# Last product of an attention-and-MLP kernel by halves of each row's tokens, one 7.5 KB place and one transfer for a step's results, and a new table of priorities

## The chip, the cores and the metric

The kernel runs on one core of a Trainium2 chip. The metric is the device time of one execution in microseconds (us). An execution's profile gives a span, from the first to the last instruction of the program; the time of the same execution lies a little above its span.

## The reference, cut to what matters

```python
# attention: x is [4, 12480, 128], inducing is [32, 128]
def mab(q, kv):
    s = scale * (q @ kv.transpose(0, 2, 1))
    a = softmax(s)                      # over the last axis, 1e-9 in the denominator
    return a @ kv
h = mab(I, x)                           # [4, 32, 128]: 32 rows look at all 12480 tokens of a batch
y = mab(x, h)                           # [4, 12480, 128]: every token looks at the 32 rows of h
# MLP on all 49920 tokens
u = y @ w_in                            # 128 -> 2048
out = (u - tanh(u)) @ w_out             # 2048 -> 128
```

The kernel uses that a token's `y` is a mixture of the 32 rows of `h`: it runs the MLP to first order around a mean on the 32 rows and then mixes 32 results per token. A check of the error's bound at the end (`limit`) would send the program to an exact general version; with these inputs that branch is not taken.

## The kernel before, in words

Data lies transposed, 128 channels on the partitions. A batch `b` (0 to 3) has six steps `s` of 1920 tokens (`SG`, four rows of 480, `NQ` = 4, `SEG` = 480) and a seventh of 1024 (four rows of 256; 64 tokens are done twice and cut off at the store by `dup`).

`first(b)`, with `attend`: for each step the tokens `xT` (7.5 KB of each partition, a buffer of the tag `xT`) are loaded and the scores against `inducing` are formed (L339, PE) and moved to SBUF (L365, DVE). After the batch's maximum is known come the exponentials (L418, ACT), their transposition to `et` (L421, DVE) and the sum over tokens (L428, PE) against the same tokens in the other layout, `xn`. Those are loaded too (`in_xn`, and `in_xl` for the seventh step), or for the steps in `TURNED` made from `xT` by PE (L401, evicted at L407).

`linear(b)`: the MLP on the 32 rows of `h` (`hT_all`): L510 up, L522, `tanh` and a series, L564 down, L568; its result is a 128x128 matrix `P4` (copied at L570), two places in turn.

`second(b, s)`, with `b_chain`: for each step again, from the same `xT` in SBUF: scores against `h` (L339, PE), transposition (L613, DVE), maximum (L615, DVE), subtraction (L620, POOL), exponential (L623, ACT), sum in two stages (L628 POOL, L631 DVE), reciprocal (L634), scaling (L635, POOL), transposition to `bt` (L639, DVE). In batch 3 every second step takes an `xn` buffer for this instead of `be` and `bt`. Then the last product (L667, PE): four matmuls with `P4`, one for each 480-token row, into two PSUM tiles `o` of two banks each. Two evictions (L673) copy the tiles to SBUF, into `ot` (batches 0 to 2) or into a spare `xT` (batch 3). There a planner may give an eviction to DVE where ACT is busy; elsewhere it is ACT's. Each half is stored by a transfer of its own (480 KB, L678; for the seventh step one transfer for both, L682).

All DMAs are issued by SP, in one order. The order of every engine's instructions comes from `Plan.order`: each operation is added with an engine, a cost, what it reads and writes, and a priority; the planner goes through time with those costs, and on each free engine starts the ready operation with the lowest priority whose buffers (`PLACES`, counted by tag) are free. Where PE would stand idle by the plan it puts matmuls of `ident` by `ident` (L763) whose result nobody reads. The priorities come from `ORD`. What an engine really waits for is a semaphore that the recording layer attaches when it sees two instructions on one tile; the planner's own picture of buffers has no part in that.

Of the kernel before, what the change touches and what calls it, by code (L numbers as in the profile page):

```python
# [10 lines left out]
F32 = mybir.dt.float32  # L11
# [8 lines left out]
NQ = 4  # L20
# [11 lines left out]
PLACES = dict(xT=11, xn=5, s1=1, be=5, bt=2, et=4, ot=5, ps=3, o=2, bs=1, D=1, M4=1, P1=2, P4=2)  # L32

ORD = dict(first=(-205, 200, 455, 875), second=(435, 945, 825, 1020), fs=(16, 32, 18, 9), ss=(21, 111, 96, 66),
           lx=(-172, -293, -302, -223), ln=(-59, -169, -75, -65), lns=(9, 15, 74, 54), turn=(60, 5, 83, 66),
           keep=(-51, -123, -93, -38), q=(-585, -579, -656, -488), half=(-201, -211, -200, -148),
           late=(230, 429, 304, 278), guard=1422, win=-364, wout=-187, lwin=-64.5, lwout=431.5,
           store=(-298, -304, -262, -383), base=(38, 76, -6, 45))
# [150 lines left out]
def fused_kernel(ctx, tc, xT, xn, xl, indT, w_in, w_out, outT):  # L189
# [17 lines left out]
    ps_o = ctx.enter_context(tc.tile_pool(name="ps_o", bufs=2, space=PSUM))  # L207
# [15 lines left out]
    plan = Plan(PLACES)  # L223
# [26 lines left out]
    add("SP", 0.3, lambda: nc.sync.dma_start(out=indT_sb, in_=indT), writes=[ind_b], pri=-500, lag=2)  # L250
# [392 lines left out]
    def second(b, s, pri):  # L643
# [3 lines left out]
        full = not dup  # L647

        def out(bt, held):

            if b == B - 1:

                whole = io_buf("xT", [C, SG])
                ots = [Buf(lambda h=h: whole.get()[:, 2 * h * seg:2 * (h + 1) * seg]) for h in range(2)]
                keep = [whole]
            elif full:
                ots, keep = [io_buf("ot", [128, NQ * HEG]) for _ in range(2)], []
            else:
                whole = io_buf("ot", [128, NQ * HEG])
                ots = [Buf(lambda h=h: whole.get()[:, 2 * h * seg:2 * (h + 1) * seg]) for h in range(2)]  # L660
                keep = [whole]
# [9 lines left out]
            for h, (o, ot) in enumerate(zip(tiles, ots)):  # L671
                def ev(copy, o=o, ot=ot):
                    copy(out=ot.get()[:, :2 * seg].rearrange("p (q n) -> p q n", q=2), in_=o.get()[:, :, :seg])  # L673
# [202 lines left out]
```

## Time and profile before

| | |
|---|---|
| time, median of 3 runs (lowest to highest) | 205.13 us (202.23 to 206.51) |
| time of the profiled execution | 204.65 us |
| its span | 202.9 us |
| busy, share of the span | PE 85%, DVE 74%, ACT 58%, POOL 45% |
| DMA | 72.3 MB in the SP queue's transfers, 91% of the 16 engines' time |
| mean granted TensorE clock | 0.957 |

A line of the views names source line, engine, operation, and output<-inputs. "x8" behind L667 are the records of four matmuls: each of these 32-bit matmuls leaves two. "landing" is the time at which a transfer's data is there, counted from its issue. Busy times are sums over the named stretch; the clock is the share of full speed that TensorE was granted in it.

### The profile page before, as it was taken

How to read it: one execution, taken by the hardware profiler on the slowest of the kernel's cores; microseconds unless marked ns; L12 is line 12 of the kernel's file. 1: busy time of each engine (PE TensorE's matmuls, PEld its weight loads, DVE VectorE, ACT ScalarE, POOL GpSimd, SP SyncE). 2: the span in 40 equal slices, each digit the busy share in tenths (PEclk: the TensorE clock that was granted, in tenths of full speed). 3: DMA queues.
4: the chain of work that ended last, by engine and by line, in shares of the span. 5: the costliest groups of instructions: out<-in, count | busy, mean ns of one | idle time of the engine just before them, and what ended most of it. 6: DMA issues, size and time to landing. Idle time of an engine off the chain costs nothing.

```text
span 202.9 us, 5388 instructions
## 1 busy us (share of the span) xinstructions
PE 172.1 (85%) x2088; PEld 98.8 (49%) x2088; DVE 149.3 (74%) x398; ACT 117.3 (58%) x236; POOL 91.1 (45%) x138
## 2 busy tenths in 40 slices
PE   7769999898689897699869889999975999899950
PEld 7634478544455543234346644344545634476530
DVE  5799499889879975286569884895772149999950
ACT  2536599534463778248765824667982297585330
POOL 1052202223659366137228532898541017899400
PEclk9969999999999999699999999999997599999996
DMA  5999999999999999979999999999999776447993
GB/s 180 400 427 421 405 423 382 411 407 417 423 368 337 363 422 403 399 282 400 351 392 424 420 414 364 371 357 414 401 286 401 316 296 246 182 181 318 404 402 121
DMA packets 15581, 72.69 MB, mean 358 GB/s; under 512 B 1856, under 2 KB 1856, under 8 KB 15552
## 3 DMA queue, kind: packets, MB, share of 16 engines
q1 hardware_dynamic: 15552, 72.31, 91.0%
q8 instruction: 17, 0.28, 0.5%
q14 instruction: 12, 0.10, 0.1%
HBM read 46.74 MB, written 25.56 MB: 356 GB/s over the span
## 4 chain that ended last, share of the span: by engine, by line
DMA 41%; PE 39%; DVE 8%; ACT 3%; SPq 2%; issue 2%; POOL 0%; DVEq 0%; ACTq 0%
DMA xT<-in_xT 29%; PE ps_m L339 12%; PE bank L428 8%; PE o L667 8%; DMA outT<-ot 5%; DMA xn<-in_xn 4%; DMA xn<-in_xl 4%; PE ps_m L401 3%; PE bank L763 3%; DVE xT L673 2%; PE ps_m L510 1%; DVE xn L302 1%; PE ps_m L522 1%; SPq L287 1%; ACT xn L407 1%
## 5 line engine op out<-in xcount | busy, mean ns | idle before, releaser
L673 ACT COPY ot<-o 128x960 f32<-128x960 f32 (+1 forms) x42 | 37.1, 910 | 19.9 <-PE o L667 10.2
L339 PE MATMUL ps_m<-xT,indT_sb 128*32 128x480 f32 (+1 forms) x224 | 28.8, 586 | 11.3 <-DMA xT<-in_xT 10.8
L428 PE MATMUL bank<-xn,et 128*32 128x128 f32 x784 | 29.8, 286 | 4.0 <-DMA xn<-in_xn 3.2
L620 POOL TENSOR_TENSOR be<-be,bmx 128x480 f32<-128x480 f32 (+1 forms) x25 | 23.8, 952 | 16.7 <-DVE bmx L615 15.4
L428 PEld LDWEIGHTS bank<-xn,et 128*32 128x32 f32 x784 | 24.0, 114 | 13.5 <-issue 4.1
L635 POOL TENSOR_TENSOR be<-be,brs 128x480 f32<-128x480 f32 (+1 forms) x25 | 23.2, 934 | 14.3 <-DVE brs L634 12.9
L667 PE MATMUL o<-bt,P 32*128 32x480 f32 (+1 forms) x200 | 28.5, 600 | 0.5 <-ACT ot L673 0.4
L763 PE MATMUL bank<-ident 128*128 128x128 f32 x176 | 26.8, 297 | 1.8 <-POOL ident masks.py:199 1.3
L365 DVE TENSOR_SCALAR_CACHE_REDUCE s<-ps_m 128x480 f32<-128x480 f32 (+1 forms) x28 | 17.3, 620 | 14.7 <-PE ps_m L339 14.7
L763 PEld LDWEIGHTS bank<-ident 128*128 128x128 f32 x176 | 23.0, 203 | 8.3 <-issue 5.7
L407 ACT COPY xn<-ps_m 128x512 f32<-128x512 f32 (+1 forms) x36 | 19.1, 565 | 13.3 <-PE ps_m L401 13.1
L339 PE MATMUL ps_m<-xT,hT_all 128*32 128x480 f32 (+1 forms) x224 | 25.1, 545 | 0.6 <-ACT D L526 0.4
L628 POOL TENSOR_TENSOR bs<-be 128x240 f32<-128x240 f32 (+1 forms) x25 | 16.9, 678 | 19.0 <-ACT be L623 13.6
L401 PE MATMUL ps_m<-ident,xT 128*128 128x128 f32 x135 | 20.6, 291 | 1.8 <-DMA xT<-in_xT 1.6
L401 PEld LDWEIGHTS ps_m<-ident,xT 128*128 128x128 f32 x135 | 15.4, 147 | 12.6 <-issue 4.1
L418 ACT ACTIVATE s<-s,nb 128x480 f32<-128x480 f32 (+1 forms) x28 | 18.9, 676 | 2.2 <-DVE nb L387 2.2
L623 ACT ACTIVATE be<-be 128x480 f32<-128x480 f32 (+1 forms) x25 | 14.5, 579 | 9.6 <-POOL be L620 9.2
L639 DVE STREAM_TRANSPOSE bt<-be 128x480 f32<-128x480 f32 (+1 forms) x25 | 15.7, 628 | 4.2 <-PE o L667 3.7
L421 DVE STREAM_TRANSPOSE et<-s 128x480 f32<-128x480 f32 (+1 forms) x28 | 17.2, 622 | 1.8 <-ACT s L418 1.5
L613 DVE STREAM_TRANSPOSE be<-ps_m 128x480 f32<-128x480 f32 (+1 forms) x25 | 15.5, 624 | 3.3 <-PE ps_m L339 3.3
L312 POOL TENSOR_TENSOR wout_sb<-wout_sb,xn 128x512 f32<-128x512 f32 x4 | 5.1, 1276 | 22.9 <-DVE xn L308 22.9
L615 DVE TENSOR_REDUCE bmx<-be 128x15 f32<-128x480 f32 (+1 forms) x25 | 14.9, 596 | 0.2
(127 smaller groups left out, 221.4 us busy)
## 6 DMA issues: line engine op xcount, KB each, us to landing
xT<-in_xT SPq DMA_DIRECT2D x24, 960.0 KB, 10.3
outT<-ot SPq DMA_DIRECT2D x39, 480.0 KB, 8.1
xn<-in_xn SPq DMA_DIRECT2D x15, 960.0 KB, 8.7
outT<-xT SPq DMA_DIRECT2D x13, 480.0 KB, 3.4
xn<-in_w_in SPq DMA_DIRECT2D x4, 512.0 KB, 5.3
xT<-in_xT SPq DMA_DIRECT2D x4, 512.0 KB, 10.5
xn<-in_w_out SPq DMA_DIRECT2D x4, 512.0 KB, 5.7
xn<-in_xl SPq DMA_DIRECT2D x4, 512.0 KB, 8.2
```

Of the source, the lines that this page charges most:

```text
L339: nc.tensor.matmul(ps[q * m:(q + 1) * m, :seg], lhsT=w, rhs=row, start=True, stop=True)
L365: nc.vector.tensor_scalar(out=s1.get()[:, s, :seg], in0=ps.get()[:, :seg], scalar1=1.0, scalar2=None, op0=ALU.mult, op1=ALU.max, accum_out ...
L401: nc.tensor.transpose(out=pt.get()[:, i * 128:(i + 1) * 128], in_=xT_b[b, s].get()[:, (k + i) * 128:(k + i + 1) * 128], identity=ident)
L407: nc.scalar.copy(out=x.get()[:, k:k + n, :].rearrange("p k c -> p (k c)"), in_=pt.get()[:, :n * 128])
L418: nc.scalar.activation(out=sl, in_=sl, func=AF.Exp, scale=SC, bias=nb.get(), accum_out=sums.get()[:, s:s + 1])
L421: add("DVE", share(0.66, seg), lambda et=et, s=s, seg=seg, kb=kb: nc.vector.transpose(out=et.get()[:, :kb].rearrange("p k i -> p (k i)"), ...
L428: nc.tensor.matmul(hacc.get()[q * m:(q + 1) * m, :], lhsT=et.get()[:, k, :], rhs=x.get()[:, k, :], start=(s == group[0] and k < NQ), stop= ...
L620: add("POOL", share(1.02, seg), lambda: nc.gpsimd.tensor_tensor(out=be.get()[:, :kb], in0=be.get()[:, :kb], in1=wide(bmx.get()[:, :kb]), o ...
L635: add("POOL", share(1.02, seg), lambda: nc.gpsimd.tensor_tensor(out=be.get()[:, :kb], in0=be.get()[:, :kb], in1=wide(brs.get()[:, :kb]), o ...
L667: nc.tensor.matmul(tiles[q // 2].get()[:, q % 2, :seg], lhsT=P4_b[b].get()[p, :], rhs=bt.get()[p, :seg], start=True, stop=True)
L673: copy(out=ot.get()[:, :2 * seg].rearrange("p (q n) -> p q n", q=2), in_=o.get()[:, :, :seg])
L763: nc.tensor.matmul(bank[:, 2 * C:2 * C + 128], lhsT=ident, rhs=ident, start=first_fill, stop=True, skip_group_check=not first_fill)
```

## The change

The last product goes by halves of each row's tokens. Half A is tokens 0 to 239 of each of the four rows, half B tokens 240 to 479. One PSUM tile `four` of four banks is made once and kept; row `q` has bank `q`, with A in columns 0 to 239 and B in columns 256 to 495. Each half has four matmuls of 240 columns and an eviction of 4x240 elements per partition. For the planner A and B are two tags, `oA` and `oB`, with one place each. Both halves of a step go into one buffer of 7.5 KB, which one transfer of 960 KB stores (480 KB for the seventh step): 28 stores in place of 52.

Places: `ot` 5 of 4 KB before, 2 of 7.5 KB now; `xT` 11 to 12, `et` 4 to 2, `bt` 2 to 3. Every entry of `ORD` but `late`, `wout` and `base` has new numbers, and the load of `inducing` (`indT_sb`) stands behind the first load of `w_in`. `PLACES`, `ORD`, this load and `second` are all that is touched; line numbers behind the first lines shift by one, and behind `second` by eleven.

```diff
-PLACES = dict(xT=11, xn=5, s1=1, be=5, bt=2, et=4, ot=5, ps=3, o=2, bs=1, D=1, M4=1, P1=2, P4=2)
+PLACES = dict(xT=12, xn=5, s1=1, be=5, bt=3, et=2, ot=2, ps=3, o=2, bs=1, D=1, M4=1, P1=2, P4=2)
-           late=(230, 429, 304, 278), guard=1422, win=-364, wout=-187, lwin=-64.5, lwout=431.5,
-           store=(-298, -304, -262, -383), base=(38, 76, -6, 45))
+           late=(230, 429, 304, 278), guard=1440, win=-361, wout=-187, lwin=-96.5, lwout=346.5,
+           store=(-298, -311, -264, -383), base=(38, 76, -6, 45))
...
-    plan = Plan(PLACES)
+    plan = Plan(dict(PLACES, oA=1, oB=1))
...
+    four = ps_o.tile([128, NQ, 512], F32, name="four")
...
         def out(bt, held):
-            if b == B - 1:
-                whole = io_buf("xT", [C, SG])
-                ots = [Buf(lambda h=h: whole.get()[:, 2 * h * seg:2 * (h + 1) * seg]) for h in range(2)]
-                keep = [whole]
-            elif full:
-                ots, keep = [io_buf("ot", [128, NQ * HEG]) for _ in range(2)], []
...
-            tiles = [Buf(lambda: ps_o.tile([128, 2, 512], F32, name="o"), "o") for _ in range(2)]
-            def pe():
-                for q in range(NQ):
-                    p = slice(q * m, (q + 1) * m)
-                    nc.tensor.matmul(tiles[q // 2].get()[:, q % 2, :seg], lhsT=P4_b[b].get()[p, :], rhs=bt.get()[p, :seg],
-                                     start=True, stop=True)
-            add("PE", share(1.05, seg), pe, reads=[bt, *held, P4_b[b]], writes=tiles, pri=pri)
-            for h, (o, ot) in enumerate(zip(tiles, ots)):
-                def ev(copy, o=o, ot=ot):
-                    copy(out=ot.get()[:, :2 * seg].rearrange("p (q n) -> p q n", q=2), in_=o.get()[:, :, :seg])
-                add("ACT", share(0.97, seg), lambda ev=ev: ev(nc.scalar.copy), reads=[o, *keep], writes=[ot], pri=pri,
-                    other=("DVE", share(1.14, seg), lambda ev=ev: ev(nc.vector.tensor_copy), pri + 1000) if b == B - 1 else None)
-                if full:
-                    at = b * N + base + 2 * h * seg
-                    add("SP", 1.2, lambda ot=ot, at=at: nc.sync.dma_start(out=outT[:, at:at + 2 * seg], in_=ot.get()[:, :2 * seg]),
-                        reads=[ot, *keep], pri=pri - of("store", b), lag=OUT_LAG)
-            if not full:
-                at = b * N + base
-                add("SP", 1.2, lambda: nc.sync.dma_start(out=outT[:, at + dup:at + NQ * seg], in_=whole.get()[:, dup:NQ * seg]),
-                    reads=[whole, *ots], pri=pri - of("store", b), lag=OUT_LAG)
+            whole = io_buf("xT" if b == B - 1 else "ot", [C, SG])
+            tiles = [Buf(lambda h=h: four[:, :, h * 256:h * 256 + seg // 2], "oAoB"[2 * h:2 * h + 2]) for h in range(2)]
+            kept = []
+            for h, o in enumerate(tiles):
+                def pe(h=h, o=o):
+                    for q in range(NQ):
+                        p = slice(q * m, (q + 1) * m)
+                        nc.tensor.matmul(o.get()[:, q, :], lhsT=P4_b[b].get()[p, :], rhs=bt.get()[p, h * seg // 2:(h + 1) * seg // 2],
+                                         start=True, stop=True)
+                def ev(copy, h=h, o=o):
+                    copy(out=whole.get()[:, :NQ * seg].rearrange("p (q n) -> p q n", q=NQ)[:, :, h * seg // 2:(h + 1) * seg // 2],
+                         in_=o.get())
+                part = Buf()
+                kept.append(part)
+                add("PE", share(0.6, seg), pe, reads=[bt, *held, P4_b[b]], writes=[o], pri=pri)
+                add("ACT", share(0.97, seg), lambda ev=ev: ev(nc.scalar.copy), reads=[o, whole], writes=[part], pri=pri,
+                    other=("DVE", share(1.14, seg), lambda ev=ev: ev(nc.vector.tensor_copy), pri + 1000) if b == B - 1 and 10 * s >= ORD.get("ev", 0) else None)
+            add("SP", 2.4 * (NQ * seg - dup) / SG, lambda: nc.sync.dma_start(
+                out=outT[:, b * N + base + dup:b * N + base + NQ * seg], in_=whole.get()[:, dup:NQ * seg]),
+                reads=[whole, *kept], pri=pri - of("store", b), lag=OUT_LAG)
```

The evictions of the last batch's middle steps, with the engines whose semaphores each waits for. The numbers behind names tell buffers apart; a row without a bracket waits for nothing that its engine has not waited for already. ACT before, from the copy of the last `P4` on (each `o_` number is a PSUM tile of two banks):

```order
L570 COPY P4_2347<-ps_m_2326 128x128 [waits PE_49]
L623 ACTIVATE be_2284<-be_2284 128x480 [waits Pool_49]
L673 COPY ot_2387<-o_2353 128x512 [waits DMAHW1_49,PE_49]
L673 COPY ot_2387<-o_2356 128x512 [waits PE_49]
L704 COPY P1_2395<-ps_m_2370 128x128 [waits PE_49]
L623 ACTIVATE xn_2328<-xn_2328 128x480 [waits Pool_49]
L673 COPY xT_2411<-o_2398 128x960 [waits PE_49]
L673 COPY xT_2411<-o_2401 128x960 [waits PE_49]
```

ACT now, from the same copy on:

```order
L571 COPY P4_2379<-ps_m_2296 128x128 [waits PE_49]
L663 COPY ot_2382<-four_81 128x4x128 [waits DMAHW1_49,Activation_49]
L663 COPY ot_2382<-four_81 128x4x128
L624 ACTIVATE xn_2326<-xn_2326 128x480 [waits DMAHW2_49,Pool_49]
L693 COPY P1_2407<-ps_m_2330 128x128
L663 COPY xT_2404<-four_81 128x4x240 [waits DVE_49]
L663 COPY ot_2426<-four_81 128x4x128 [waits DMAHW2_49,PE_49,Activation_49]
L663 COPY ot_2426<-four_81 128x4x128
```

DVE evicts half A of the step `xT_2404` and ACT its half B, and ACT's copy waits for DVE; before, both copies of `xT_2411` were ACT's and waited for PE. Between the copies of `M4` (L513, now L514) and of this `P4` ACT had 3 whole evictions and 2 of a seventh step; now 8 whole ones stand there.

PE now, the last product of three steps of batch 3 (before, the two tiles of a step each had their own waits, and a product's first matmul waited for the tile of the step before):

```order
L659 MATMUL four_81<-bt_2423,P4_2379 128x240 [waits DVE_49,Activation_49]
L659 MATMUL four_81<-bt_2423,P4_2379 128x240 x3
L752 MATMUL bank_80<-ident_70 128x128
L659 MATMUL four_81<-bt_2423,P4_2379 128x240 [waits Activation_49]
L659 MATMUL four_81<-bt_2423,P4_2379 128x240 x3
L752 MATMUL bank_80<-ident_70 128x128 x2
L659 MATMUL four_81<-xn_2299,P4_2379 128x240 [waits DVE_49,Activation_49]
L659 MATMUL four_81<-xn_2299,P4_2379 128x240 x7
L752 MATMUL bank_80<-ident_70 128x128 x2
L659 MATMUL four_81<-bt_2485,P4_2379 128x240 [waits DVE_49]
L659 MATMUL four_81<-bt_2485,P4_2379 128x240 x3
```

Each semaphore of these rows stands for the instruction ahead of it on the other engine that last touched `four`, A or B: half B of `bt_2423` waits for the eviction of its half A, and both halves of `xn_2299`, which stand together, for the last eviction of the step before.

SP's queue around the last load of all, `in_xl` of batch 3, before:

```order
L678 DMA outT<-ot_1840 128x960
L411 DMA xn_1889<-in_xn 128x1920
L411 DMA xn_1920<-in_xn 128x1920
L678 DMA outT<-ot_1931 128x960
L678 DMA outT<-ot_1947 128x960
L411 DMA xn_1983<-in_xn 128x1920
L411 DMA xn_2029<-in_xn 128x1920
L678 DMA outT<-ot_2008 128x960
L678 DMA outT<-ot_2050 128x960
L411 DMA xn_2108<-in_xl 128x1024
```

and now:

```order
L670 DMA outT<-ot_1759 128x1920
L412 DMA xn_1848<-in_xn 128x1920
L412 DMA xn_1885<-in_xn 128x1920
L412 DMA xn_1920<-in_xn 128x1920
L670 DMA outT<-ot_1813 128x1920
L412 DMA xn_1989<-in_xn 128x1920
L412 DMA xn_2033<-in_xl 128x1024
L670 DMA outT<-ot_2031 128x1920
```

In all, 27 stores of 480 KB stood ahead of that load; now 11 of 960 KB and one of 480 KB do. In the order of the program 16 whole evictions and 6 of a seventh step stood behind the last sum over tokens (L428 of that load's tokens); now 21 and 6 do.

More of the change, by code (lines that the diff above doesn't have):

```diff
@@ L206, in fused_kernel @@
     ps_s = ctx.enter_context(tc.tile_pool(name="ps_s", bufs=1, space=PSUM))
-    ps_o = ctx.enter_context(tc.tile_pool(name="ps_o", bufs=2, space=PSUM))
+    ps_o = ctx.enter_context(tc.tile_pool(name="ps_o", bufs=1, space=PSUM))
     io_scope = tc.tile_pool(name="io", bufs=1)
```

13 lines of the change are left out of this document (4 added, 9 removed).

## The prediction

> **What bounds the kernel now.** I read the page's head and its groups first, then the stretches, then the timeline of the end. In the stretches the columns are length, busy time of PE, PE's weight loads, DVE, ACT and POOL, then clock, DMA share and GB/s.
>
> ```profile
> span 202.9 us, 5388 instructions
> q1 hardware_dynamic: 15552, 72.31, 91.0%
> 2.20:158.80 156.60, 136.13 (x1755) 78.39 (x1757) 117.86 (x319) 93.51 (x197) 69.73 (x100) 0.97 0.99 388
> 158.80:203.00 44.20, 35.16 (x337) 19.52 (x331) 30.46 (x72) 22.52 (x38) 20.64 (x32) 0.92 0.68 270
> ```
>
> Up to 158.8 us the DMA engines are 99% busy and no compute engine is over 87% (136.13 of 156.60): transfers bound this part, and it ends when the last load has landed. The other 44 us are a tail in which no engine is full. The timeline gives its landmarks:
>
> ```profile
> 150.39 1.03 SPq L411 DMA_DIRECT2D xn<-in_xl  x1
> xn<-in_xl SPq DMA_DIRECT2D x1, 512.0 KB, 8.9
> 161.68 0.65 PE L428 MATMUL bank<-xn,et 128*32 128x128 f32 x16
> 164.72 1.06 PE L510 MATMUL ps_m<-win_sb,hT_all 128*32 128x512 f32 x8
> 176.02 0.28 ACT L570 COPY P<-ps_m 128x128 f32<-128x128 f32 x1
> 178.63 1.45 PE L667 MATMUL o<-bt,P 32*128 32x480 f32 x8
> 183.90 1.09 DVE L673 COPY xT<-o 128x960 f32<-128x960 f32 x1
> 183.98 0.94 ACT L673 COPY xT<-o 128x960 f32<-128x960 f32 x1
> 195.53 0.58 ACT L673 COPY xT<-o 128x512 f32<-128x512 f32 x1 [1.37 <-PE o L667]
> 196.14 0.33 SPq L682 DMA_DIRECT2D outT<-xT  x1
> outT<-xT SPq DMA_DIRECT2D x3, 480.0 KB, 4.4
> ```
>
> The last load, issued at 150.39, lands 8.9 later, at 159.3; the last sum over tokens starts at 161.68 (I call this T0). Then the MLP: `P4` of batch 3 is copied at T0+14.3, the first product of batch 3 starts at T0+17.0, and the last eviction ends at 196.11, T0+34.4. The last three stores land 4.4 (their median) after their issue, the last of them issued at 196.14; from the last eviction to the span's end it is 202.9 − 196.1 = 6.8. The tail's pace is in the chain:
>
> ```profile
> 185.15 1.03 PE o L667 x8
> 186.20 1.17 DVE xT L673
> 187.37 0.04 issue
> 187.42 1.16 PE o L667 x8
> 188.60 0.95 DVE xT L673
> ```
>
> A step costs product plus one eviction, 185.08 to 187.42, some 2.3 us, because ACT and DVE evict the two tiles of a step side by side (183.90 and 183.98 above).
>
> **The change, part by part.** *The hand-over of `four`.* The code names one tile, and the order's waits show what follows: half B's first matmul waits for the eviction of half A, the next step's product for the last eviction, and where the two evictions of a step are on two engines, ACT's waits for DVE's. Nothing that touches `four` overlaps anything else that does. The durations:
>
> ```profile
> L673 ACT COPY xT<-o 128x960 f32<-128x960 f32 x7 | 6.6, 954 | 4.1 <-PE o L667 4.1
> L673 DVE COPY xT<-o 128x960 f32<-128x960 f32 x5 | 5.7, 1145 | 0.0
> L673 ACT COPY xT<-o 128x512 f32<-128x512 f32 x1 | 0.6, 585 | 1.4 <-PE o L667 1.4
> L673 DVE COPY xT<-o 128x512 f32<-128x512 f32 x1 | 0.7, 691 | 0.7 <-PE o L667 0.7
> 185.08 1.09 PE L667 MATMUL o<-bt,P 32*128 32x480 f32 x8
> 176.55 0.71 PE L667 MATMUL o<-bt,P 32*128 32x256 f32 x8
> ```
>
> A half evicts 4x240 = 960 elements, as a tile did: 0.95 on ACT, 1.15 on DVE. Four matmuls of 240 columns have no row; they lie between half of 1.09 (0.55) and the 0.71 of four with 256 columns. I take 0.68, near the upper row, which has almost its size. A step in series is then 2 x (0.68 + 0.95) = 3.3 us, against 2.3.
>
> *Middle.* Up to the last load some 11 such steps (36 us) lie in over 100 us in which the DMA engines never stand still. PE's in-order waits for half A's eviction, 11 x 0.95 = 10 us, fit into the 20 us that PE is not busy there. I cost them at nothing; if that cover is gone, they are the 10 us. The `inducing` load behind `w_in` and the other counts of `et` and `bt` lie under the same 0.99, at nothing to 0.5 us.
>
> *Load phase.* What stands ahead of the last load in SP's queue shrinks. Before, 27 half stores did (27 x 480 KB = 13.3 MB); now 11 whole ones and one of 480 KB (11.3 MB). With loads unchanged that is 2.0 MB less, and at 388 GB/s 5.1 us. So the load lands near 159.3 − 5.1 = 154.2. The bounds are 0 (if DMA falls idle meanwhile, as it would if `ot`'s two places starve it) and 5.1; I take the whole, since 0.99 is a row that speaks for a transfer-bound queue. How long two places may stall is bounded by nothing and by what five places of half the size cost so far:
>
> ```profile
> ACT ot L673 <- PE o L667: 10.2, 6, 3.6
> ACT ot L673 <- DMA outT<-ot: 9.5, 7, 3.8
> ```
>
> *From the load to T0.* The whole store ahead of that load (`ot_1813`) must land before its place is evicted into again. It lands two loads, 1.5 MB or 3.9 us at 388 GB/s, before the last one. Behind it the program's order has three evictions (2.85), three half products (2.0) and some 0.5 of L428 ahead of the last sum: 5.4. T0 is therefore 154.2 + 5.4 − 3.9 = 155.7, against 161.68: 6.0 earlier.
>
> *From T0 to the last eviction.* All products and evictions left form one chain. Ahead of it about 1.3 of a wait for a store's landing (worked out from `ot_2031`'s place in the queue). Evictions: 21 whole ones lie behind T0 by the order and one at it; 19 on ACT, 3 on DVE: 19 x 0.954 + 3 x 1.145 = 21.6. Six of seventh steps: 5 x 0.585 + 0.691 = 3.6. Products: 12 halves of 0.68 (8.2), four steps whose halves stand together at 1.09 (4.4), three seventh steps at 0.71 (2.1); the products of the first two evictions lie at or ahead of T0. That is 1.3 + 21.6 + 3.6 + 14.7 = 41.2, and some 41 hand-overs at 0.04 each (the row "187.37 0.04 issue" in the chain above, between an eviction and a product) make 42.8.
>
> Into this chain fall pieces that ACT or PE do between two links, in their order, so that the chain stands still:
>
> ```profile
> 164.72 1.06 PE L510 MATMUL ps_m<-win_sb,hT_all 128*32 128x512 f32 x8
> L691 ACT ACTIVATE xT<-wout_sb 128x1024 f32<-128x1024 f32 x2 | 2.1, 1070 | 0.0
> 177.39 0.61 ACT L623 ACTIVATE be<-be 128x480 f32<-128x480 f32 x1 [1.09 <-POOL be L620]
> 168.35 0.37 ACT L526 COPY D<-ps_m 128x256 f32<-128x256 f32 x1
> ```
>
> The up product is 1.06 (0.9 not hidden); the MLP's small ACT work (two copies of 0.37 and the tanh beside them) 1.0; one pass of L691 with the copies at 0.28 about 1.4; two exponentials of 0.61 each, 1.2; the copy of `P4` 0.28, and a wait for DVE 0.4. They add to 5.2; the bounds are 0 and that sum, and I take 5.0, because ACT waits in order and has these rows ahead of evictions. The last eviction then ends at T0 + 47.8 = 203.5, where it was T0+34.4 = 196.1.
>
> *The end.* Stores now come one per 3.3 us. In the tail before they came faster than they left:
>
> ```profile
> 186.00:201.00 15.00, 9.21 (x74) 5.92 (x70) 9.21 (x22) 4.68 (x6) 3.57 (x5) 0.94 0.91 357
> DMA to landing us min/median/max: 2.5/5.8/13.9
> ```
>
> At 357 GB/s a store of 983 KB takes 2.8, so no queue is left at the end, and the last store should land in the shortest time of this tile, 2.5. Before, 6.8 − 4.4 − 0.05 leaves 2.3 for what follows a landing; I take 1.7, since 4.4 is the median of the last three, and a store that queues behind two others lands later than that. So 0.05 + 2.5 + 1.7 = 4.2.
>
> **Sum:** 155.7 + 47.8 + 4.2 = 207.7 of span. The profiled execution took 204.65, 1.75 more than its span, so 209.4 us, 2.3% above 204.65. The median of the runs is 205.13 and their spread 2%; a kernel of this kind shows a change of about 2% and no less.
>
> A rule of the skill bears on the hand-over. The Trainium skill, "PSUM — Partial Sum Buffer", section "PSUM bank collisions raise a hardware error", says that two engines on one bank in the same partitions at once raise an error even at different columns, and that guards go by bank and not by address. By it the two halves, which share all four banks, can't overlap however they are declared (209.4); without it they could (the third rival, 195.6). No run here shows a shared bank so far.
>
> **The rivals.** *PE's clock falls in the tail, which makes it slower still.* The trace shows that it can:
>
> ```profile
> 150.00:155.00 5.00, 2.54 (x40) 1.41 (x38) 2.86 (x7) 3.12 (x8) 1.69 (x2) 0.97 0.88 328
> 155.00:160.00 5.00, 4.23 (x66) 3.86 (x66) 0.04 (x1) 1.27 (x2) 0.46 (x1) 0.50 0.99 398
> 159.85 1.90 PE L667 MATMUL o<-bt,P 32*128 32x480 f32 x8
> ```
>
> After a stretch in which PE was busy half of the time its clock is 0.50, and a product takes 1.90 for 1.09. In series PE works 1.4 of each 3.3 us of a tail step, less than that half, if the fillers of L763 don't bridge the gap. 0.8 more in ten steps is 8: 217, and 213 where it catches half of them. It decides from the point where PE's gaps are as long as those of 150 to 155. The Trainium skill, "TensorE: Matmul & The Clock Gate", section "What's actually happening", states that the clock halves after an idle window of about 3.4 us; with gaps of 1 us this rival would cost nothing by it. The two rows neither bear that out nor speak against it, being averages of 5 us.
>
> *Not slower: the chain goes at its bare sum.* If the 5.2 of in-order pieces hide beside the chain (they overlap what the other engine does) and the half product is nearer 0.55 (12 x 0.13 = 1.6 less), the span is 207.7 − 5.0 − 1.6 = 201.1 and the time 202.9, or 205 with half of the pieces. It decides where ACT's pieces fall into PE's products rather than between product and eviction. For it speaks that a product leaves ACT 0.68 free; against it that L691 takes 1.07.
>
> *The halves overlap, as the diff describes them.* Then a step is bound by ACT and DVE side by side or by PE, some 2.0 us instead of 2.3. A faster step against a new order with more evictions behind T0: I leave the end where it was, T0+34; with the end's 4.2 that gives 155.7 + 34 + 4.2 = 193.9, a time of 195.6 (−4.4%). Against it stand the waits in the order, which name the other half's instruction.
>
> **How the numbers follow.** Forecast 0.55 (205 to 213), clock 0.15 (213 to 219), bare sum 0.20 (202 to 205), overlap 0.10 (195 to 198). The prediction is 209.4. For 8 in 10 the range leaves out the overlap and the upper part of the clock's case: 200.5 to 215.5. The bounds of 2% are 200.6 and 208.7 against 204.65. Slower than that are the clock and 0.35 of the forecast's 0.55: 0.50. Within are the other 0.20 of it and most of the bare sum: 0.35. Faster: 0.15, overlap and a bare sum with a shorter gate.
>
> **What would show it.** The last load issued 5 us earlier, T0 near 156; evictions of a tail step that never overlap, and a step of 3.1 to 3.3 us; the first product of batch 3 some 22 after T0; the last eviction near 203 to 204, the last store's landing near 2.5. Wrong would be: DMA below 0.95 before the last load (`ot`'s places starve it, T0 not earlier, +6); ACT idle less than 1 us per tail step (overlap); rows of L667 with 1.9 behind T0 (clock); or a first product of batch 3 nearer T0+17 (the pieces and the earlier batch's steps are not in the chain).

## The result, and the profile after

The changed kernel took 225.88 us (median of 6 runs, 223.48 to 232.04), the kernel before 205.09 beside it. The ratio is 1.1001 with a 95% interval of 1.0879 to 1.1123: 10% slower, where 2.3% was forecast and 215.5 us was the upper end of the range. The direction was right, the size was not. The profiled execution took 225.99 us. Some executions of each kernel ran at a lower clock and took longer: a ratio and its interval leave these out, a median does not.

The page's head and its slices, after:

```profile
span 224.2 us, 5700 instructions
PE   7669996789869997959969996987699875876780
PEclk9969999699979999996979999999799999557557
DMA  6999989999998999999999999899673766645742
q1 hardware_dynamic: 12096, 72.31, 83.8%
```

The bytes are the same (72.31 MB). Two things stand out against before: the clock's row has four fives among its last six slices, and the part in which DMA is full ends no earlier than before, at about 157 us. The landmarks, from the timeline:

```profile
153.82 0.33 SPq L412 DMA_DIRECT2D xn<-in_xl  x1
164.98 0.65 PE L429 MATMUL bank<-xn,et 128*32 128x128 f32 x16
186.03 0.27 ACT L571 COPY P<-ps_m 128x128 f32<-128x128 f32 x1
187.33 1.09 PE L659 MATMUL four<-bt,P 32*128 32x240 f32 x16 [0.31 <-ACT ot L663]
218.88 0.58 ACT L663 COPY xT<-four 128x512 f32<-128x512 f32 x1 [4.19 <-DVE xT L663]
xn<-in_xl SPq DMA_DIRECT2D x1, 512.0 KB, 7.8
```

The last load is issued at 153.82 and lands at 161.6. T0, the last sum over tokens, is at 164.98, 3.3 us later than before instead of 6.0 earlier. The first product of batch 3 starts 22.35 us behind it, the last eviction ends at 219.46. Set against the forecast's three terms, in us:

| | forecast | measured | difference |
|---|---|---|---|
| T0 | 155.7 | 165.0 | +9.3 |
| T0 to the last eviction | 47.8 | 54.5 | +6.7 |
| last eviction to the span's end | 4.2 | 4.7 | +0.5 |
| span | 207.7 | 224.2 | +16.5 |

Of the 9.3 at T0, 7.4 are the load's landing (161.6 for 154.2) and 1.9 the way from there to T0 (3.4 for 1.5). So there are two questions: why the gate, which is what T0 is called below, is late, and what the 6.7 of the tail are. The chain of waits after has an entry for each:

```profile
144.91 13.18 DMA outT<-ot
158.16 0.97 ACT ot L663
159.17 0.69 PE four L659 x8
159.86 0.73 PE bank L752 x2
160.58 1.86 PE bank L429 x30
...
199.42 1.18 PE four L659 x8
200.60 1.15 PE bank L752 x4
201.75 1.96 PE four L659 x16
203.73 0.97 ACT xT L663
204.72 1.16 DVE xT L663
```

Ahead of T0 an eviction waits for a store that needed 13.18 us from issue to landing. In the tail, halves take 1.18 and two halves together 1.96, where 0.69 and 1.09 are their durations at full clock (the first from 186.88 us in the run e5_warm below, the second at 187.33 above).

### The profile page after: what moved, and what is told of

It is laid out like the page before. It is cut to its first block, busy times and chain, and to the rows that moved or that the text cites. A ratio compares the mean times of both kernels' runs of the same rounds, so it can differ in the third digit from the quotient of the medians.

```text
span 224.2 us, 5700 instructions
## 1 busy us (share of the span) xinstructions
PE 182.7 (82%) x2268; PEld 111.4 (50%) x2268; DVE 145.6 (65%) x396; ACT 119.6 (53%) x238; POOL 92.1 (41%) x138
## 3 DMA queue, kind: packets, MB, share of 16 engines
q1 hardware_dynamic: 12096, 72.31, 83.8%
## 4 chain that ended last, share of the span: by engine, by line
PE 33%; DMA 30%; DVE 14%; ACT 13%; issue 5%; POOL 3%; SPq 1%; ACTq 0%; DVEq 0%
DMA outT<-ot 19%; PE four L659 10%; PE ps_m L340 9%; ACT ot L663 8%; PE bank L429 6%; DMA xn<-in_w_out 5%; ACT xT L663 4%; DMA xT<-in_xT 3%; DMA xn<-in_w_in 3%; PE ps_m L402 3%; DVE xn L303 2%; DVE xT L663 2%; PE bank L752 2%; PE ps_m L523 1%; DVE xn L309 1%
## 5 line engine op out<-in xcount | busy, mean ns | idle before, releaser
L663 ACT COPY ot<-four 128x960 f32<-128x960 f32 (+1 forms) x42 | 36.9, 909 | 29.3 <-PE four L659 15.1
L659 PE MATMUL four<-bt,P 32*128 32x240 f32 (+1 forms) x400 | 32.9, 420 | 18.1 <-ACT ot L663 12.6
L429 PE MATMUL bank<-xn,et 128*32 128x128 f32 x784 | 31.6, 293 | 3.4 <-DVE et L422 2.1
L659 PEld LDWEIGHTS four<-bt,P 32*128 32x128 f32 x400 | 17.6, 204 | 31.6 <-ACT ot L663 18.1
L429 PEld LDWEIGHTS bank<-xn,et 128*32 128x32 f32 x784 | 25.4, 117 | 11.0 <-issue 3.2
L752 PE MATMUL bank<-ident 128*128 128x128 f32 x132 | 27.3, 356 | 1.9 <-POOL ident masks.py:199 1.3
L340 PE MATMUL ps_m<-xT,hT_all 128*32 128x480 f32 (+1 forms) x224 | 27.6, 574 | 0.1
L629 POOL TENSOR_TENSOR bs<-be 128x240 f32<-128x240 f32 (+1 forms) x25 | 16.5, 659 | 24.5 <-ACT be L624 16.6
L408 ACT COPY xn<-ps_m 128x512 f32<-128x512 f32 (+1 forms) x36 | 19.3, 559 | 12.3 <-PE ps_m L402 12.2
L402 PE MATMUL ps_m<-ident,xT 128*128 128x128 f32 x135 | 22.2, 307 | 0.2
L402 PEld LDWEIGHTS ps_m<-ident,xT 128*128 128x128 f32 x135 | 16.6, 155 | 10.2 <-issue 4.3
L663 ACT COPY xT<-four 128x960 f32<-128x960 f32 (+1 forms) x10 | 9.1, 922 | 19.6 <-PE four L659 7.8
```

The lines of the kernel that those rows point to most:

```text
L340: nc.tensor.matmul(ps[q * m:(q + 1) * m, :seg], lhsT=w, rhs=row, start=True, stop=True)
L402: nc.tensor.transpose(out=pt.get()[:, i * 128:(i + 1) * 128], in_=xT_b[b, s].get()[:, (k + i) * 128:(k + i + 1) * 128], identity=ident)
L408: nc.scalar.copy(out=x.get()[:, k:k + n, :].rearrange("p k c -> p (k c)"), in_=pt.get()[:, :n * 128])
L429: nc.tensor.matmul(hacc.get()[q * m:(q + 1) * m, :], lhsT=et.get()[:, k, :], rhs=x.get()[:, k, :], start=(s == group[0] and k < NQ), stop= ...
L659: nc.tensor.matmul(o.get()[:, q, :], lhsT=P4_b[b].get()[p, :], rhs=bt.get()[p, h * seg // 2:(h + 1) * seg // 2], start=True, stop=True)
L663: copy(out=whole.get()[:, :NQ * seg].rearrange("p (q n) -> p q n", q=NQ)[:, :, h * seg // 2:(h + 1) * seg // 2], in_=o.get())
```

## The experiments

Two theories stood at the start: **hand-over** (one tile puts products and evictions in series) and **numbers** (the new table delays loads and stores whatever the tiles do). The clock's part of the tail and the two places came up on the way. For each run the times are medians of four (of six in the first two rows), and ratios are against runs of the kernel before on the same chip, whose median lay between 203.2 and 205.1. T0 and the stretch behind it (to the last eviction's end) are from each run's one profile:

| kernel | time, us | ratio (95%) | T0 | stretch |
|---|---|---|---|---|
| before | 205.1 | 1 | 161.7 | 34.4 |
| changed | 225.9 | 1.100 (1.088 to 1.112) | 165.0 | 54.5 |
| e1_two_tiles | 211.6 to 234.9 | none | 165.8 | 54.1 |
| e2_old_numbers | 218.3 | 1.071 (1.055 to 1.087) | 169.8 | 41.8 |
| e3_new_numbers | 209.6 | 1.033 (1.017 to 1.049) | 165.9 | 34.9 |
| e4_two_tiles_old_numbers | 213.3 | 1.055 (1.041 to 1.070) | 168.4 | 36.7 |
| e5_warm | 224.3 | 1.098 (1.086 to 1.110) | 164.5 | 53.0 |
| e6_three_places | 215.3 | 1.057 (1.048 to 1.066) | 160.2 | 45.9 |
| e7_one_tile | 207.8 | 1.010 (1.000 to 1.020) | 162.6 | 40.4 |
| e8_whole_stores | 208.8 | 1.018 (1.005 to 1.030) | 167.3 | 33.7 |
| e9_fillers_in_gaps | 220.3 | 1.079 (1.069 to 1.089) | 166.0 | 48.2 |
| e10_three_places_gaps | 212.0 | 1.044 (1.032 to 1.057) | 156.3 | 46.1 |
| e11_two_tiles_gaps | 218.9 to 230.3 | none | 169.5 | 53.1 |
| e12_three_places_old_numbers | 217.1 | none | 171.4 | 37.6 |
| e13_four_places_before | 207.5 | 1.022 (1.015 to 1.029) | 163.5 | 35.0 |

Where the table says none, no ratio was taken. The old table of priorities goes with `xT` 11, `et` 4 and `bt` 2 in e2 and e4, the new one with `et` 2 and `bt` 3 in e3.

### The tiles and the numbers

**e1_two_tiles**, the changed kernel with

```diff
-    four = ps_o.tile([128, NQ, 512], F32, name="four")
+    pair = [ps_o.tile([128, 2, 512], F32, name=f"pair{h}") for h in range(2)]
...
-                    for q in range(NQ):
+                    for q in (2 * h, 2 * h + 1):
...
-                        nc.tensor.matmul(o.get()[:, q, :], lhsT=P4_b[b].get()[p, :], rhs=bt.get()[p, h * seg // 2:(h + 1) * seg // 2],
+                        nc.tensor.matmul(o.get()[:, q % 2, :], lhsT=P4_b[b].get()[p, :], rhs=bt.get()[p, :seg],
```

> The changed kernel with its halves cut the other way: half A is rows 0 and 1 of a step, half B rows 2 and 3 (two matmuls of 480 columns each), each half in a PSUM tile of its own. Order, places, numbers and whole stores stay; only the waits between A and B go. Theory 'hand-over' (products and evictions of one tile in series cost the time): from the last sum to the last eviction 54.5 us falls to about 40, PE's clock stays at 1.0 in the tail, the 60 to 160 us stretch wins back 1 to 1.5 MB (3 to 4 us); time about 205 to 210. Rival 'numbers' (the new order and two places delay loads and stores whatever the tiles do): only the tail's overlap comes back, the last load stays near 154 and the time stays at 215 or more.

Its four runs took 211.57, 227.44, 234.58 and 234.85 us, at mean clocks of 0.968, 0.883, 0.854 and 0.846. The profiled one (227.44) has 54.1 us in the stretch, so the tail's overlap did not show as time there; the fastest lies 12 us under the fastest run of the changed kernel. Neither expectation is met by that spread, and the other cut of the halves turned out to change more than waits: two matmuls of 480 columns take 1.07 (the first row from e11 below), as long as four do, so a step's product takes 2.14 instead of 1.09.

**e2_old_numbers**, **e3_new_numbers** and **e4_two_tiles_old_numbers** exchange the tables:

```diff
-           lx=(-172, -291, -302, -287), ln=(-60, -169, -75, -64), lns=(9, 15, 74, 53), turn=(100, 35, 123, 106),
+           lx=(-172, -293, -302, -223), ln=(-59, -169, -75, -65), lns=(9, 15, 74, 54), turn=(60, 5, 83, 66),
...
-    add("SP", 0.3, lambda: nc.sync.dma_start(out=indT_sb, in_=indT), writes=[ind_b], pri=ORD["lwin"] + 0.5, lag=2)
+    add("SP", 0.3, lambda: nc.sync.dma_start(out=indT_sb, in_=indT), writes=[ind_b], pri=-500, lag=2)
```

(two of the places where they differ; all of `ORD` is exchanged, with the counts that are named, and e3 is the reverse exchange in the kernel before).

> The changed kernel with one tile of four banks and whole stores, but the table of priorities, the place of the inducing load and the places of xT, et and bt of before. Theory 'hand-over': nothing is gained, 222 to 230, since the old order counts on overlap too. Rival 'numbers': the first 60 us read 18.8 MB again instead of 17.3 (3.8 us), and the time is 215 to 220.

> The kernel before with its two tiles per step and half stores, but the new table, the new place of the inducing load, et 2 and bt 3 (xT 11 and ot 5 as before). Theory 'hand-over': within 2% of before, 201 to 209. Rival 'numbers': the first 60 us lose 1.5 MB (3.8 us) as in the changed kernel and the time is 209 or more.

> Both: halves by rows in a tile each, whole stores with two places of 7.5 KB, and the old table. Theory 'hand-over': 200 to 207, like before or a little less, since 2 MB of stores fall behind the last load. Rival 'two places starve the evictions': 210 or more, with evictions waiting for stores to land for over 9.5 us in all.

e2 came out at 218.3, where the numbers theory had put it, but not by its mechanism: T0 is at 169.8, not earlier but 5 us later than in the changed kernel, and the gain is the stretch of 41.8, with 16 whole evictions behind T0 against the changed kernel's 22. e3 shows that the new table with its `et` and `bt` costs 3.3%, with T0 4.2 later and the stretch unchanged; its order, planned for two tiles and half stores, has 15 whole evictions behind T0, so the late evictions of the changed kernel do not come from the table alone. e4 against e2 has 5.1 us less in the stretch (36.7 against 41.8), with the same evictions behind T0. That is the overlap of two tiles less their longer products, and some of it may be the clock, which was 1.00 in e4's stretch and 0.96 in e2's. Evictions wait 19.2 us for stores, its rival's sign.

The numbers theory as stated fell: with one tile and whole stores the old table gives a later gate than the new one. The order of the transfers shows why. In the one that the old table gives with whole stores, 14 of 960 KB and one of 480 KB stand ahead of the last load (e2, e4 and e12), 14.3 MB; the new table leaves 11.3 MB there. The 2.9 MB between them are 7.6 us at 388 GB/s. A table and the size of the stores belong together.

### One tile by itself

**e7_one_tile**, the kernel before with

```diff
-            tiles = [Buf(lambda: ps_o.tile([128, 2, 512], F32, name="o"), "o") for _ in range(2)]
+            tiles = [Buf(lambda h=h: four[:, 2 * h:2 * h + 2, :], "o") for h in range(2)]
```

> The kernel before, with one PSUM tile of four banks in place of two tiles of two from a pool of two; rows 0 and 1 and rows 2 and 3 are evicted as before, order of all engines, table, places and half stores stay. Only the waits on the tile are added. Theory 'hand-over': a step of the tail goes from 2.3 to 3.2 us (product 1.09, then 0.95 and 1.15 one after the other), the last eviction comes 6 to 10 us later, 211 to 217 (more if the clock falls). Rival 'hidden': within 2%, 201 to 209.

Its chain of waits in the tail:

```profile
187.42 1.13 PE four L668 x8
188.57 1.17 DVE xT L674
189.76 0.97 ACT xT L674
190.77 1.13 PE four L668 x8
191.93 0.97 ACT xT L674
192.92 1.17 DVE xT L674
194.13 1.13 PE four L668 x8
```

Product, one eviction, the other eviction, next product: a step takes 3.35 us (187.42 to 190.77, and 190.77 to 194.13) instead of 2.3. The stretch grew by 6.0 us, at clock 1.00 in both kernels, as the hand-over theory has it, but the time only by 1.0% (the theory's 211 to 217 was missed by a good 3 us). The kernel before gives 6.8 us to draining stores behind its last eviction; here it is 207.5 − 202.95 = 4.55, with the last store landing 3.4 behind its issue instead of 4.4. A third of the stretch's loss came back there. The profiled execution (209.31) was the slowest of the four, and 4.7 above that of before; the ratio of 1.010 says less, and its interval reaches 1.

### The clock in the tail

**e5_warm** puts three matmuls of `ident` (fillers, whose result nobody reads) behind each half's product of batch 3, and leaves out the planner's own from there on:

```diff
+                    if b == B - 1:
+                        fills(3)
...
-        if not any(a < op.start < z for a, z in quiet):
+        if not warm and not any(a < op.start < z for a, z in quiet):
```

> The changed kernel, with three matmuls of ident by ident straight behind each half's product of batch 3 (a result that nobody reads), and from there on none of the planner's own fillers. Theory 'clock': PE's clock stays at 1.0 behind the first product of batch 3, products take 0.69 and 1.09 again instead of 1.18 and 1.98, the stretch from the last sum to the last eviction falls from 54.5 to about 47, the time to 216 to 219. Rival 'series alone': the clock has no part in the length of the tail, the fillers only add work, 225 or more.

The clock stayed up in nearly all of the tail (0.97 in the stretch), yet the stretch lost only 1.5 us, and the time of 224.3 lies far above the 216 to 219 expected. The timeline shows why:

```profile
202.57 0.69 PE L666 MATMUL four<-xn,P 32*128 32x240 f32 x8 [0.21 <-ACT xT L672]
203.19 0.94 PE L648 MATMUL bank<-ident 128*128 128x128 f32 x6
204.05 0.69 PE L666 MATMUL four<-xn,P 32*128 32x240 f32 x8
204.81 0.96 ACT L672 COPY xT<-four 128x960 f32<-128x960 f32 x1 [2.29 <-PE four L666]
```

Where both halves stand ahead of the evictions, the first eviction waits for the second half too, and the fillers between them (0.94) stand on the path.

**e9_fillers_in_gaps** therefore puts fillers behind the last sum only where an eviction separates a product from PE's next instruction, and none of the planner's there (from its edit):

```diff
+        if op in products and op.start > last_sum:
+            rest = ops[ops.index(op) + 1:]
+            k = next((k for k, x in enumerate(rest) if x.eng == "PE"), 0)
+            for _ in range((0, 2, 5)[min(2, sum(x in copies for x in rest[:k]))]):
+                nc.tensor.matmul(bank[:, 2 * C:2 * C + 128], lhsT=ident, rhs=ident, start=False, stop=True, skip_group_check=True)
```

> The changed kernel with its fillers behind the last sum moved: two matmuls of ident by ident behind a product that one eviction follows before PE's next instruction, five where two follow, none elsewhere, and none of the planner's there. In e5_warm the clock stayed up, but three fillers stood between the two halves of four steps whose evictions wait for both, some 0.8 us each. Theory 'clock and fillers': with fillers only in gaps the stretch from the last sum to the last eviction is 45 to 48 (53.0 in e5_warm, 54.5 in the changed kernel) and the time 216 to 219. Rival 'the series alone makes the tail': 53 or more, 223 to 226.

The same view of the two kernels, changed and then e9_fillers_in_gaps, over each one's stretch (length, busy time of PE, its loads, DVE, ACT, POOL, then clock, DMA share, GB/s):

```profile
165.00:219.50 54.50, 42.71 (x418) 25.31 (x414) 28.47 (x71) 28.21 (x45) 22.72 (x35) 0.78 0.57 229
```

```profile
166.00:214.20 48.20, 38.93 (x458) 24.36 (x454) 28.44 (x71) 28.20 (x45) 22.97 (x36) 0.98 0.63 254
```

DVE, ACT and POOL do the same work in both (28.47 and 28.44, 28.21 and 28.20, 22.72 and 22.97); the clock is 0.98 instead of 0.78, and the stretch from T0 to the last eviction is 6.3 us shorter. The time only fell to 220.3, a little over what was expected, since T0 was 1.0 later in this profile. Clock and fillers together are the 6.3, and this run does not divide them: among them are 14 records of fillers that took 3.35 us, at half clock, in front of the last product of the changed kernel, 2.2 of it behind the eviction that the product could have followed:

```profile
213.60 3.35 PE L752 MATMUL bank<-ident 128*128 128x128 f32 x14
213.73 0.96 ACT L663 COPY xT<-four 128x960 f32<-128x960 f32 x1 [3.82 <-DVE limit L729]
216.88 1.14 PE L659 MATMUL four<-bt,P 32*128 32x128 f32 x16
```

**e11_two_tiles_gaps** is e1_two_tiles with the fillers of e9.

> e1_two_tiles (each half two rows, in a tile of its own, all else as changed) with the fillers in gaps. Its runs spread from 211.6 to 234.9 with clocks from 0.97 to 0.85. Theory 'clock': the slow ones go, 207 to 213, and the difference to e9_fillers_in_gaps is what the waits on one tile cost at full clock, 4 to 9 us. Rival: the spread stays.

The spread stayed (218.89, 227.50, 228.44 and 230.34 us), as the rival had it. The clock was 1.00 from 186.5 us on, where the fillers stand, and half for 20 us ahead of them. The first row is a product at full clock, the second the stretch of half clock:

```profile
159.01 1.07 PE L661 MATMUL pair<-bt,P 32*128 32x480 f32 x4 [0.59 <-ACT ot L665]
164.40:185.00 20.60, 20.12 (x104) 7.30 (x104) 6.60 (x19) 8.28 (x16) 7.48 (x15) 0.50 0.28 115
```

What separate tiles are worth in the new order at full clock therefore stays open; in the old order it is 5.1 (e2 to e4, with the reservations above) to 6.0 (before to e7) in the stretch.

### Places and the gate

**e6_three_places**, the changed kernel with `xT=11, ot=3` in place of `xT=12, ot=2`; **e10_three_places_gaps** adds the fillers of e9; **e12_three_places_old_numbers** has the old table as well.

> The changed kernel with ot 3 places and xT 11 instead of 2 and 12, all else the same (the planner's order follows). Theory 'two places stall': evictions wait for stores for less than 5 us in all instead of 13.3, the last sum over tokens comes 3 to 5 us earlier than 165, time 219 to 222 if the clock falls in the tail as it did. Rival 'places don't matter': last sum at 164 to 166 and 224 to 228.

> Three places (ot 3, xT 11) and the fillers in gaps, in the changed kernel. In e6_three_places the clock stayed up without them and the stretch was 45.9. Theory 'clock and fillers': nothing more is to be had, 212 to 216. Rival 'fillers help as such': under 211.

> The changed kernel with three places (ot 3, xT 11) and the old table and place of the inducing load. Theory 'places and numbers both delay the last load': the first 60 us read over 18 MB (17.1 in e6_three_places), the last sum comes 2 to 4 us before that of e6_three_places (160.2), time 209 to 213. Rival 'the old table doesn't fit whole stores': last sum at 161 or later, 214 or more, as two places with the old table gave 169.8.

The waits of evictions for stores, changed and then e6_three_places (total, times, longest):

```profile
ACT ot L663 <- DMA outT<-ot: 13.3, 6, 3.9
```

```profile
ACT ot L663 <- DMA outT<-ot: 4.2, 3, 2.1
```

And the rates of the transfers (last column) up to 60 us and from 60 to 150 us, before, then changed, then e6_three_places, then e10_three_places_gaps:

```profile
2.00:60.00 58.00, 50.30 (x615) 32.50 (x618) 48.76 (x123) 32.08 (x74) 16.67 (x23) 0.97 1.01 405
60.00:150.00 90.00, 80.45 (x1060) 41.62 (x1050) 66.43 (x191) 57.04 (x115) 50.91 (x75) 0.98 0.99 379
```

```profile
2.00:60.00 58.00, 49.25 (x525) 32.56 (x528) 44.15 (x114) 27.41 (x61) 14.02 (x15) 0.94 0.97 376
60.00:150.00 90.00, 78.28 (x1108) 44.63 (x1104) 62.50 (x184) 54.45 (x115) 47.59 (x75) 0.94 0.97 363
```

```profile
2.00:60.00 58.00, 50.23 (x545) 33.66 (x548) 45.17 (x114) 28.18 (x62) 15.18 (x20) 0.94 0.97 371
60.00:150.00 90.00, 78.80 (x1123) 43.81 (x1112) 64.15 (x188) 57.10 (x119) 48.37 (x72) 0.98 0.98 385
```

```profile
2.00:60.00 58.00, 49.50 (x569) 32.63 (x572) 47.71 (x120) 29.08 (x65) 17.12 (x22) 0.97 0.99 390
60.00:150.00 90.00, 79.64 (x1200) 44.80 (x1192) 66.67 (x191) 59.38 (x124) 48.33 (x72) 1.00 0.97 384
```

With three places T0 comes at 160.2 and 156.3, with two at 165.0, 164.5 and 166.0 (changed, e5, e9): 6.9 us earlier on the mean. Between e9 and e10, which ran on the same chip with the same fillers, the times differ by 8.2 us, and the intervals of their ratios lie apart. From 60 to 150 us the three places move 22 GB/s more than the two; over 90 us that is 2.0 MB, 5.1 us at the 388 GB/s of before. In e6 the clock stayed up by itself, so that its time fell below what was expected; e10 is at the lower end of its range. Both have 20 whole evictions and 5 of a seventh step behind T0, where the changed kernel has 22 and 6. Between these two the stretch is the same (45.9 and 46.1) and T0 differs by 3.9, which nothing in the edit explains: so much the gate scatters, and 2.8 of it fit the first 60 us (371 and 390 GB/s, 1.1 MB).

The first 60 us, which hold loads and no stores, are a loss of their own, which the places do not explain: with three of them e6 moves 371 GB/s there and e10 390, with the same order. The rates are 383 to 405 in the seven profiles with the old table (405 before) and 362 to 390 in the eight with the new one (376 in the changed kernel, 382 in e3, where the table is all that is new but for `et` and `bt`). From 405 to 376 is 1.7 MB, 4.3 us at 388 GB/s. Which of the new numbers does it was not tried.

e12 went its rival's way: T0 at 171.4 with the old table. There evictions wait only 6.6 us for stores, against 15.1 with two places in e2, and yet the middle moves 363 GB/s in e12 and 362 in e2: what the third place gives is shown with the new table alone.

**e13_four_places_before** takes one of five places from the kernel before (`ot=4`).

> The kernel before with ot 4 places of 4 KB (two steps' worth, as in the changed kernel) instead of 5; half stores, two tiles and the table stay. Theory 'two steps' worth of places delays the last load': evictions wait for stores for more than the 9.5 us of before, the last sum over tokens comes 2 to 5 us behind 161.7, time 207 to 211. Rival 'only whole stores make two places short': last sum within 1 us of 161.7, 202 to 206.

Evictions waited 12.3 us for stores instead of 9.5, T0 moved by 1.8, which is less than the gate scatters, and the time by 2.2% (1.5 to 2.9): room for two steps costs something with half stores too, less than was expected of T0. With two places and `xT` 11 the planner finds no order under the new table, so the 6.9 cannot be split between `ot` and `xT`.

**e8_whole_stores** gives the kernel before whole stores, three places, and `et` 2:

```diff
-                if full:
-                    at = b * N + base + 2 * h * seg
-                    add("SP", 1.2, lambda ot=ot, at=at: nc.sync.dma_start(out=outT[:, at:at + 2 * seg], in_=ot.get()[:, :2 * seg]),
+            add("SP", 2.4 * (NQ * seg - dup) / SG, lambda: nc.sync.dma_start(
+                out=outT[:, b * N + base + dup:b * N + base + NQ * seg], in_=whole.get()[:, dup:NQ * seg]),
```

> The kernel before with whole stores alone: three places of 7.5 KB, one transfer of 960 KB behind both evictions of a step, et 2 to make room; its two PSUM tiles and its table stay. Theory of the prediction (fewer bytes ahead of the last load): the last sum over tokens comes up to 5 us earlier, 199 to 204. Rival 'whole stores hold places longer': evictions wait for stores for more than 9.5 us, the last sum comes later than 161.7, 206 to 212.

T0 came 5.6 later, the contrary of what was expected, though evictions waited less for stores (7.8 us) than before. So the rival's time was met and its cause was not. But the edit did not do what the theory asked for, because the order was planned anew with whole stores. Ahead of the last load e8 issues

```profile
outT<-ot SPq DMA_DIRECT2D x15, 960.0 KB, 9.6
outT<-ot SPq DMA_DIRECT2D x1, 480.0 KB, 5.2
```

which is 15.2 MB where before had 13.3. The 2.0 MB more are 5.1 us at 388 GB/s: the gate moved as the bytes ahead of the last load did, only the other way. That speaks for the theory and not against it.

## Why the prediction was right or wrong

- **The hand-over** was right. Nothing that touches `four` overlaps. The half product took 0.69 for the 0.68 taken, and in e9's chain a step whose halves stand apart is twice 0.73 and 0.97, 3.5 with its hand-overs, for the forecast's 3.3. e7_one_tile's step of 3.35 is made up otherwise (one product of 1.13, evictions of 0.97 and 1.17), so that its nearness to 3.3 proves only the series. The overlap rival (0.10) is out.
- **The tail's length was right at full clock, in part by luck.** e9_fillers_in_gaps has 48.2 us where the sum gave 47.8, and the first product of batch 3 came 22.35 behind T0 in the changed kernel, for some 22. (The 45.9 and 46.1 of e6 and e10 are for fewer evictions.) The bare-sum rival is out as well. But "All products and evictions left form one chain" does not hold for the first part. From 168 to 180.8 us e9's chain runs over PE, through products and the MLP; in the changed kernel it runs from 167 to 179.1 through the MLP on PE, DVE and POOL. Four whole evictions lie beside it in both, 3.9 us that the sum had counted. What the chain holds there besides products (scores, the MLP, fillers and 1.0 of issue) is 9.5 us in e9, where the sum took 5.0 for all such pieces. The two errors nearly cancelled. The 20.1 us that the stretch grew by divide into 6.0 for one tile (e7 against before), 6.3 for clock and fillers (changed against e9), and a rest of 7.8, which no run shows by itself. An estimate for it is 5 x (0.95 + 0.68) = 8.2, for the five whole evictions that the new order has behind the gate beyond the 17 of before, each with its product.
- **The clock rival came true** and had been given 0.15. It was priced at 8 and cost 6.3 with the fillers' share. The step that failed is its odds. Its own sum was near (PE busy for 1.4 of 3.3 us), but the chance went by gaps of 1 us and by fillers that bridge them. At the place where the clock fell the gaps were longer (the two stretches lie on either side of the fall):

```profile
187.10:190.50 3.40, 1.41 (x18) 1.01 (x18) 1.95 (x3) 1.58 (x4) 2.60 (x4) 1.00 0.73 289
190.50:193.90 3.40, 2.63 (x26) 2.06 (x30) 2.61 (x14) 1.59 (x4) 1.90 (x3) 0.50 0.72 296
```

  PE was busy for 1.41 of 3.40 us while two evictions of one step went one after the other on DVE and ACT (PE's gap ahead of the next product, at 190.76, was 2.02), and then the clock was half. The Trainium skill, "TensorE: Matmul & The Clock Gate", section "What's actually happening", has the clock fall after an idle window of about 3.4 us. Here the 3.4 us ahead of the fall were not empty: PE was idle for 59% of them, and by that rule, as the prediction read it, nothing would have been lost.
- **T0 was wrong by 9.3, the largest miss.** The step is "With loads unchanged that is 2.0 MB less, and at 388 GB/s 5.1 us", and then "I take the whole, since 0.99 is a row that speaks for a transfer-bound queue". Its bytes were right: 11.3 MB stand ahead of the last load, e8 with 15.2 MB has a later gate, and in e10, with three places, the load lands at 155.4 and T0 is at 156.3, for 154.2 and 155.7. What failed is the rate, which was held at 388. From 2 us to its landing the changed kernel moved 365 GB/s where the kernel before moved 387: 1.7 MB less than before in the first 60 us and 1.4 MB less from 60 to 150. At 388 GB/s these are 4.3 and 3.7 us, near the 7.4 by which the load landed late.

  The second part is the one that three places give back (385 and 384 for 363). The text had named it, "as it would if `ot`'s two places starve it", bounded it at 0 gain, and left it out of the cases. That bound was also no bound: what was lost here is more than the change gained, and T0 came 3.3 later than before. The first part it had put "at nothing to 0.5 us", as the `inducing` load and the other counts, and the new numbers of the table not at all; e3 shows 382 GB/s for 405 there. The sign that it gave for a starved queue, DMA below 0.95, did not show it either: the share up to 150 us was 0.97. The rate fell more than the share. From the load's landing to T0 it was 3.4 for 1.5, with the 13.18 us of the store that the eviction waited for.
- **The middle was rightly costed at nothing.** Up to T0 PE's weight loads for a half did wait for evictions, much as the 10 us of the forecast had it. From 60 to 150 us, changed and then e10_three_places_gaps:

```profile
PEld four L659 <- ACT ot L663: 12.2, 10, 2.4
```

```profile
PEld four L661 <- ACT ot L665: 10.5, 12, 2.3
```

  But e10 waits nearly as long and has its gate within 0.6 us of the forecast. So waits of this length do not by themselves delay the gate.
- **The end** was right in kind: 4.7 for 4.2, with 3.6 for the last landing instead of 2.5. e7 shows the same, with a third of the slower tail given back.
- **The table's own cost was not in the sum.** e3_new_numbers is 3.3% slower with two tiles and half stores: 29 half stores for 27 stand ahead of its last load (1.0 MB, 2.5 us), and the first 60 us are slower. With whole stores the new table is a gain on the whole (T0 at 160.2 against 171.4 with three places), since it leaves 2.9 MB fewer ahead of the last load, so the 3.3% do not add to the rest.

## What to carry to other kernels

A resource that is shown 99% busy covers other work only as long as the change does not feed it worse: count the bytes ahead of the last load in the order that is really planned, then ask separately whether the rate holds, in GB/s and not in busy share, from the first transfers on. Count the places that each transfer needs, and let the starved case be a case with a price beyond zero. Where a change puts two engines in series on one buffer, the engine that now idles may lose its clock, as PE did here, and its later work is priced at the lower one; look at its longest gap, not at the mean of its step. A slower tail gives part of its loss back where stores were queuing behind it. One profile's gate can lie 4 us from another's of the same order, so small moves of it prove little.

## What was not expected of the hardware

- PE's clock did not come back for 20 us while PE was busy for 20.12 of 20.60 us (e11, above). The products there work on two of a step's four rows at a time: two matmuls took 1.07 where four take 1.09. In e9, with four at a time, the clock was 0.98 behind the gate with PE busy for 38.93 of 48.20 us. But such products do not by themselves bring the clock down, since e4, which has the same ones, kept it up through its whole stretch:

```profile
168.38:205.12 36.74, 33.77 (x290) 16.79 (x288) 25.35 (x64) 23.46 (x39) 20.04 (x31) 1.00 0.61 252
```

  Whether they keep it from coming back once it has fallen was not tried.
